# Soft-MoE dispatch after attention: the sum of weights as a 513th column, a minimum on GpSimd, left logits copied by ScalarE, and a new order

## The chip, the cores and the metric

The kernel runs on one NeuronCore of a Trainium2 chip. The core has five engines with a queue each, which meet only through semaphores: PE (TensorE, matrix products, with weight loads shown apart as PEld), DVE (VectorE), ACT (ScalarE), POOL (GpSimd) and SP (SyncE, which here only issues DMA transfers). Each engine executes its queue in the order in which the program was built. The metric is the device time of one execution in microseconds, as the median of several runs.

## The reference

The input is an attention block with a batch of 8, 8 heads, 576 positions and a head width of 64, followed by a soft mixture of experts. All data are float32.

```python
scores = scale * np.matmul(q, k.transpose(0, 1, 3, 2))
thresh = np.max(scores, axis=-1, keepdims=True) - tau
scores = np.where(scores >= thresh, scores, -1000000000.0)
attn = softmax(scores);  x = (attn @ v), laid out as 4608 tokens x 512
logits = x @ phi                              # 4608 x 32 slots
d = np.exp(logits - logits.max(0));  d /= d.sum(0) + 1e-09
slot_input = d.T @ x                          # 32 x 512
for e in range(8): slot_out[e] = np.maximum(slot_input[e] @ w1[e], 0.0) @ w2[e]
c = np.exp(logits - logits.max(1));  c /= c.sum(1) + 1e-09
return c @ slot_out
```

The softmax `d` runs over all 4608 tokens of a slot. The kernel forms it batch by batch: it keeps a running extreme of the logits, a running sum of weights and a running weighted sum of x, and rescales both sums when the extreme moves.

## The kernel before, in words

Attention is done for 32 pairs of heads (`pair(p)`, L1350), four pairs to a batch. A pair has nine row tiles. For each, PE multiplies queries by keys (L1423, L1428 for the last tile) into a PSUM region; DVE copies the scores negated to SBUF and takes their minimum with them (L1435); ACT exponentiates (L1447); POOL computes the threshold from the minimum (`thr`, L1450); DVE masks the exponentials by the threshold and sums them (L1453); PE transposes the result (L1323), ACT copies it out (L1328), and PE multiplies by the values (L1569, L1581, L1594). Only PE, DVE and ACT reach PSUM; there are four regions of two banks for everything (`REGIONS = 4`).

After the fourth pair of a batch comes `dispatch(b)` (L1667). PE computes the logits of the batch for 32 slots (L1688), four column groups wide. DVE copies them negated and takes their minimum (`l4` and one column of `M`, L1694). For every batch but the first, a DVE reduction over the two columns of `M` gives the new running minimum (L1698), and ACT computes the factor `f` by which older sums shrink (L1700). ACT exponentiates the logits (L1702) to weights `dT`, PE transposes them, ACT copies them to `d`. The logits themselves are transposed too and stored for the later softmax over slots: ACT copies those of the 512 main positions (L1712), DVE those of the 64 left positions (L1714), both from one region.

`weigh` (L1731) then forms a weighted sum: four products beside each other and smaller ones for left positions (L1738, L1743), and one DVE operation that merges the region into an accumulator, a copy for the first batch (L1749), else old times `f` plus new (L1751). It is called once with a column of ones, for the sum of weights (`csum`, 128x1, L1754), and once with x (`acc`, 128x512); for the last batch the second is cut into two halves of 256 columns. Each call takes a PSUM region of its own.

After the last dispatch the sums are normalized (`scale`, `slot_in`), and the tail begins: eight experts in two groups (`stage1` L1944, `stage2` L1987), whose weights SP loads. Thirteen slots are filled in small pieces during attention (L1283); the rest is loaded in whole units (L1297, L1302, L1304), each as soon as the buffers that it overwrites are free. The last step combines and writes the output (`combine`).

The order of all this is not the order of the code. `Order.add` records every operation with its engine, an estimated duration, its buffers and a due time. `plan` (L1062) picks again and again the engine whose next operation can start first; among the operations of one engine the due time decides, and due times come from `TABLE`, a table of some thousand numbers by scope and index. It also assigns the PSUM regions and buffer slots. `run` then emits the operations in that order. So a change of the table or of one operation moves neighbours on every engine.

## Time and profile before

| what | value |
|---|---|
| device time, median of 3 runs | 527.16 us (526.46 to 528.51) |
| device time of the profiled execution | 527.1 us |
| its span, first to last instruction | 525.3 us |
| busy in the span: PE / DVE / ACT / POOL | 508.0 / 466.1 / 449.1 / 274.2 us |
| attention, 13.1 to 450 us: PE / DVE / ACT / POOL busy | 435.96 / 427.35 / 415.02 / 259.73 us |
| granted PE clock, mean of the span | 0.991 |

The span is about 1.8 us shorter than the device time, which also holds what lies around the first and last instruction. The attention part, with seven of the eight dispatches in it, fills the first 450 us. From about 452 to 491 us the DMA engines are full with expert weights, and the rest is the last products and the output. A group line of the profile gives a source line, engine, operation and shape, the count, then busy time and mean duration, then the idle time of the engine just before these instructions and what ended it.

### The profile page before, as it was taken

The numbers are of one execution on the slowest core, as the hardware profiler recorded it, in microseconds if no ns is written. First come the engines' busy times: TensorE is split into PE (matmuls) and PEld (weight loads), VectorE is DVE, ScalarE is ACT, GpSimd is POOL, SyncE is SP. The second block draws the span as 40 slices with busy tenths as digits, with TensorE's granted clock in tenths as the row PEclk, the third lists the DMA queues.
The fourth block names the chain that finished last, engine by engine and source line by source line (L and its number), as shares of the span: only waits on it lengthen the run. The fifth ranks groups of instructions, "written<-read, shape, count | busy, mean of one in ns | idle before, by whom it ended". The sixth has DMA issues, their size and how long they took to land.

```text
span 525.3 us, 26986 instructions
## 1 busy us (share of the span) xinstructions
PE 508.0 (97%) x11367; PEld 404.2 (77%) x11367; DVE 466.1 (89%) x1316; ACT 449.1 (85%) x759; POOL 274.2 (52%) x476
## 2 busy tenths in 40 slices
PE   8999999999999999999999999999999999999881
PEld 5778888878978887888788888888788888643361
DVE  6999998999999999999999999999999999623372
ACT  3899998999999998999899989999999999622272
POOL 2555674465656665656466545765466646121110
PEclk9999999999999999999999999999999999999987
DMA  6344553474356533554665553653645334999598
GB/s 170 90 122 105 142 137 99 117 179 126 93 134 162 146 81 98 159 129 133 168 159 144 144 125 106 190 149 96 181 106 161 84 93 138 371 418 416 203 374 345
DMA packets 47817, 86.62 MB, mean 165 GB/s; under 512 B 11344, under 2 KB 31440, under 8 KB 46160
## 3 DMA queue, kind: packets, MB, share of 16 engines
q1 hardware_dynamic: 47376, 84.45, 54.3%
q8 instruction: 89, 1.46, 1.2%
q10 hardware_dynamic: 320, 0.44, 0.3%
q14 instruction: 32, 0.26, 0.2%
HBM read 75.43 MB, written 9.44 MB: 162 GB/s over the span
## 4 chain that ended last, share of the span: by engine, by line
PE 90%; DMA 2%; DVE 2%; ACT 2%; issue 1%; POOL 0%; DVEq 0%; POOLq 0%; ACTq 0%
PE ps L1423 25%; PE ps L1569 21%; PE ps L1323 19%; PE ps L1594 4%; PE ps L1428 4%; PE ps L1581 3%; PE h L1944 3%; PE ps L1688 2%; DMA w<-in_w 2%; PE ps L1630 2%; PE ps L1738 2%; PE o L2038 2%; PE ps L1536 1%; DVE ss L1435 1%; PE so L1987 1%
## 5 line engine op out<-in xcount | busy, mean ns | idle before, releaser
L1435 DVE TENSOR_SCALAR_CACHE_REDUCE ss<-ps 128x576 f32<-128x576 f32 x288 | 208.4, 750 | 8.2 <-PE ps L1423 3.4
L1450 POOL TENSOR_SCALAR thr<-nmx,pabs 128x1 f32<-128x1 f32 x288 | 146.4, 514 | 123.7 <-DVE ss L1435 119.8
L1453 DVE SCALAR_TENSOR_TENSOR p<-ss,thr,p 128x576 f32<-128x576 f32 x256 | 203.9, 821 | 0.5 <-POOL thr L1450 0.2
L1447 ACT ACTIVATE p<-ss,nmx 128x576 f32<-128x576 f32 x256 | 190.2, 786 | 11.5 <-DVE ss L1435 10.3
L1423 PE MATMUL ps<-k,q 64*128 64x288 f32 x1024 | 158.0, 425 | 0.7 <-DVE k L1387 0.7
L1323 PEld LDWEIGHTS ps<-ident,p 64*128 64x128 f32 x2304 | 91.5, 138 | 18.3 <-issue 3.0
L1423 PEld LDWEIGHTS ps<-k,q 64*128 64x128 f32 x1024 | 86.5, 188 | 23.1 <-ACT pTa L1328 2.3
L1323 PE MATMUL ps<-ident,p 64*128 64x64 f32 x2304 | 101.8, 223 | 0.3 <-ACT pTa L1328 0.2
L1328 ACT COPY pTb<-ps 128x1024 f32<-128x1024 f32 (+1 forms) x96 | 83.4, 881 | 2.6 <-PE ps L1323 2.1
L1328 ACT COPY pTa<-ps 128x1024 f32<-128x1024 f32 x64 | 65.4, 1023 | 1.7 <-PE ps L1323 1.4
L1569 PE MATMUL ps<-pTb,vv 64*64 64x128 f32 x1984 | 61.1, 270 | 0.0
L1569 PE MATMUL ps<-pTa,vv 64*64 64x128 f32 x1984 | 60.5, 271 | 0.0
L1569 PEld LDWEIGHTS ps<-pTb,vv 64*64 64x64 f32 x1984 | 56.3, 133 | 2.4 <-ACT pTb L1328 0.5
L1569 PEld LDWEIGHTS ps<-pTa,vv 64*64 64x64 f32 x1984 | 54.8, 133 | 2.8 <-DVE ss L1435 1.0
L1625 POOL TENSOR_TENSOR x<-x,ri 128x512 f32<-128x512 f32 x31 | 38.0, 1225 | 14.1 <-ACT x L1328 12.4
L1478 POOL TENSOR_SCALAR pL<-pL,ri 128x576 f32<-128x576 f32 x31 | 27.6, 891 | 14.7 <-DVE ri L1477 11.0
L1387 POOL TENSOR_SCALAR k<-k,flag 128x576 f32<-128x576 f32 x31 | 29.7, 959 | 2.6 <-PE ps L1323 1.4
L1328 ACT COPY pTl<-ps 128x256 f32<-128x256 f32 x64 | 27.9, 436 | 0.9 <-PE ps L1323 0.8
L1581 PE MATMUL ps<-pTl,vv 64*64 64x128 f32 x496 | 27.0, 278 | 0.0
L1608 ACT COPY xT<-ps 128x256 f32<-128x256 f32 x62 | 23.5, 379 | 4.1 <-PE ps L1594 1.9
L1447 ACT ACTIVATE pL<-ss,nmx 128x576 f32<-128x576 f32 x32 | 25.3, 791 | 1.8 <-DVE ss L1435 1.8
L1453 DVE SCALAR_TENSOR_TENSOR pL<-ss,thr,pL 128x576 f32<-128x576 f32 x32 | 26.0, 814 | 0.1
(194 smaller groups left out, 638.0 us busy)
## 6 DMA issues: line engine op xcount, KB each, us to landing
q<-in_qT SPq DMA_DIRECT2D x62, 288.0 KB, 4.0
w<-in_w SPq DMA_DIRECT2D x52, 256.0 KB, 3.9
host<-in_w SPq DMA_DIRECT2D x10, 1024.0 KB, 8.9
k<-in_kT SPq DMA_DIRECT2D x62, 144.0 KB, 3.9
vv<-in_vt SPq DMA_DIRECT2D x62, 128.0 KB, 3.5
out<-host SPq DMA_DIRECT2D x9, 768.0 KB, 4.3
w<-in_w SPq DMA_DIRECT2D x5, 1024.0 KB, 9.2
vx<-in_vt SPq DMA_DIRECT2D x62, 64.0 KB, 2.9
```

Of the source, the lines that this page charges most:

```text
L1323: nc.tensor.transpose(out=s[:, g, c:c + 64], in_=ins[g], identity=ident[rows[g], rows[g]], tile_position=(64 * g, 0))
L1328: G.add("ACT", 51 + 0.833 * n, nom, lambda: nc.scalar.copy(*io()), r, w)
L1387: sc = lambda e, kc=kc: lambda: e.tensor_scalar(out=kt.t[:, kc], in0=kt.t[:, kc], scalar1=flag8, **one)
L1423: nc.tensor.matmul(s.t[:, g, 0:HS], qt.t[rows[g], h, c * 128:(c + 1) * 128], kt.t[rows[g], h * HS:(h + 1) * HS], start=True, stop=True, ti ...
L1435: dve(678, t + OFF['mx'], [s], [ss, nmx], lambda s=s, ss=ss, nmx=nmx: nc.vector.tensor_scalar(out=ss.t.rearrange("p (a k) -> p a k", a=2), ...
L1447: G.add("ACT", 684, t + OFF['ex'], lambda sv=sv, nmx=nmx, view=view: nc.scalar.activation(view(), sv(), AF.Exp, bias=nmx.t, scale=-1.0), [ ...
L1450: pool(250, t + OFF['th'], pre=75, fn=lambda nmx=nmx, thr=thr: nc.gpsimd.tensor_scalar(out=thr.t, in0=nmx.t, scalar1=1.0, scalar2=pabs, op ...
L1453: fn=lambda sv=sv, thr=thr, view=view, i=i: nc.vector.scalar_tensor_tensor(out=view(), in0=sv(), scalar=thr.t, in1=view(), op0=ALU.is_le, ...
L1478: pool(725, t + OFF['sc'], lambda: nc.gpsimd.tensor_scalar(out=pL.t[:, SL:SL + S], in0=pL.t[:, SL:SL + S], scalar1=ri.t[:, 8:9], **one), [ ...
L1569: nc.tensor.matmul(area(w, h, l)[rows[a]], vv.t[rows[h], n * 64:(n + 1) * 64], pT.t[rows[h], n // 4, n % 4, a * 128:(a + 1) * 128], tile_p ...
L1581: nc.tensor.matmul(area(ab[l], h, l)[rows[a]], vv.t[rows[h], SM:S], pTl.t[rows[h], (l * 2 + a) * 128:][:, 0:128], tile_position=(64 * h, 6 ...
L1625: G.add("POOL", 1040, u + 6.8, own=f"new{j}" + group(b), r=[ri], w=[x[j]], fn=lambda: nc.gpsimd.tensor_tensor(out=wide(), in0=wide(), in1= ...
```

## The change

There are four edits. The two accumulators become one tile `sums` of 513 columns, `acc` and `csum` being views of it. For all batches but the last, the call of `weigh` for the sum of weights goes; its five products now stand ahead of those for x, write the first column of the second bank of the same region, and one DVE operation merges 513 columns. The smaller of the two minima is taken by a POOL `tensor_scalar` instead of a DVE reduction. The logits of the left positions are copied by ACT instead of DVE. And the table of due times is new in nearly every entry; two of its lines are shown here.

```diff
--- before.py
+++ after.py
@@ -57,926 +57,923 @@
 TABLE = {}
 for _n, _v in (
     ("load", [
-        75668,
+        72728,
     ]),
...
@@ -1233,8 +1230,8 @@
     lmain = [lall[:, row(b):row(b) + 4] for b in range(B)]
     lleft = lall[:, N9 - 1:NR:N9]
     crow = cp.tile([128, NR], F32, name="crow")
-    acc = cp.tile([128, DM], F32, name="acc")
-    csum = cp.tile([128, 1], F32, name="csum")
+    sums = cp.tile([128, DM + 1], F32, name="sums")
+    acc, csum = sums[:, 0:DM], sums[:, DM:]
     rs = cp.tile([128, 1], F32, name="rs")
     stn = cp.tile([128, 32], F32, name="stn")
     nabs = cp.tile([128, 1], F32, name="nabs")
@@ -1695,8 +1692,9 @@
             out=l4.t[:, 0:192], in0=lone(wl)[:, 0:192], scalar1=-1.0, scalar2=3.4028234663852886e38, op0=ALU.mult, op1=ALU.min,
             accum_out=M.t[:, 0:1] if b else new.t[:, 1:2]))
         if b > 0:
-            dve(69, u + 1.4, [M], [new["run"]], lambda: nc.vector.tensor_reduce(
-                out=new.t[:, 1:2], in_=M.t, axis=AX.X, op=ALU.min))
+            G.add("POOL", 250, u + 1.4, lambda: nc.gpsimd.tensor_scalar(
+                out=new.t[:, 1:2], in0=M.t[:, 0:1], scalar1=M.t[:, 1:2], scalar2=1.0, op0=ALU.min, op1=ALU.mult),
+                [M], [new["run"]], pre=75)
             G.add("ACT", 200, u + 1.5, lambda: nc.scalar.activation(
                 f.t, M.t[:, 1:2], AF.Exp, bias=new.t[:, 1:2], scale=-1.0), [M["run"], new["run"]], [f])
         G.add("ACT", 319, u + 1.6, lambda: nc.scalar.activation(
@@ -1711,8 +1709,8 @@
         ptr(2, u + 2.5, [l4], [w], lambda w=w: both(w, l4))
         G.add("ACT", 158, u + 2.8, lambda w=w: nc.scalar.activation(
             lmain[b].rearrange("p (g c) s -> p g (c s)", g=2), w.t[:, :, 0:64], AF.Copy, scale=-1.0), [w], [lm[b]])
-        dve(215, u + 2.9, [w], [ll[b]], lambda w=w: nc.vector.tensor_scalar(
-            out=lleft[pl, b // 2], in0=w.t[rows[1], 0, 64:64 + NS], scalar1=-1.0, scalar2=None, op0=ALU.mult))
+        G.add("ACT", 110, u + 2.9, lambda w=w: nc.scalar.activation(
+            lleft[pl, b // 2], w.t[rows[1], 0, 64:64 + NS], AF.Copy, scale=-1.0), [w], [ll[b]])
         if b == B - 1:
 
             w = Buf("s")
@@ -1728,12 +1726,17 @@
                 fs[:, 1:2], new.t[:, 1:2], AF.Exp, bias=fs[:, 0:1], scale=-1.0), [new["run"], fb[0]], [fb[1]])
             dve(96, u + 5.8, [fb[1]], [sb], lambda: nc.vector.tensor_scalar(
                 out=msel[:, 0], in0=st1, scalar1=fs[:, 1:2], scalar2=None, op0=ALU.mult))
-        def weigh(c0, cn, n, rhs, lrhs, dst, pd, dur, nom):
+        def weigh(c0, cn, n, rhs, lrhs, dst, pd, dur, nom, total=False):
 
 
             w = bank_of(b == B - 1)
+            area = lambda: w.t.rearrange("p a n -> p (a n)")[:, 0:n + total]
 
             def mm(w=w):
+                for c in range(5 if total else 0):
+                    nc.tensor.matmul(
+                        w.t[c % 4 * 32:c % 4 * 32 + 32, 1, 0:1], d.t[:, c * NS:(c + 1) * NS], ones_left if c == 4 else ones,
+                        start=c < 4, stop=c > 0, tile_position=(0, 32 * (c % 4)), skip_group_check=True)
                 for c in range(4):
                     nc.tensor.matmul(
                         lone(w)[c * 32:(c + 1) * 32, 0:n], d.t[:, c * NS:(c + 1) * NS], rhs(c), start=True,
@@ -1746,12 +1749,15 @@
             rd = ([] if n == 1 else [x, xl]) + [d]
             G.add("PE", dur, nom, mm, rd, [w], mode=COLS4, more=116 if n > 1 else -60)
             if b == 0:
-                dve((65 if n > 1 else 126) + n * 1.17, nom + 1, [w], [pd], lambda: nc.vector.tensor_copy(dst, lone(w)[:, 0:n]))
+                dve((65 if n > 1 else 126) + n * 1.17, nom + 1, [w], pd, lambda: nc.vector.tensor_copy(dst, area()))
             else:
-                dve((65 if n > 1 else 126) + n * 1.17, nom + 1, [w, f], [pd], lambda: nc.vector.scalar_tensor_tensor(
-                    out=dst, in0=dst, scalar=f.t, in1=lone(w)[:, 0:n], op0=ALU.mult, op1=ALU.add))
-
-        weigh(0, 1, 1, lambda c: ones, lambda c: (slice(0, 1), ones_left), csum, cs, 192, u + 6)
+                dve((65 if n > 1 else 126) + n * 1.17, nom + 1, [w, f], pd, lambda: nc.vector.scalar_tensor_tensor(
+                    out=dst, in0=dst, scalar=f.t, in1=area(), op0=ALU.mult, op1=ALU.add))
+
+        if b == B - 1:
+            weigh(0, 1, 1, lambda c: ones, lambda c: (slice(0, 1), ones_left), csum, [cs], 192, u + 6)
+        else:
+            G.skip(2)
         pieces = 2 if b == B - 1 else 1
         n = 512 // pieces
         if pieces == 2:
@@ -1759,8 +1765,8 @@
         for g in range(pieces):
             q = slice(g * n, (g + 1) * n)
             weigh(g * 2, 4 // pieces, n, lambda c, q=q: x.t[:, c, q], lambda c, q=q: (
-                slice(c * 128 - q.start, c * 128 + 128 - q.start), xl.t[:, c * 128:c * 128 + 128]), acc[:, q],
-                ac[g] if pieces == 2 else ac, 1101 / pieces, u + 7)
+                slice(c * 128 - q.start, c * 128 + 128 - q.start), xl.t[:, c * 128:c * 128 + 128]), acc[:, q] if pieces == 2 else sums,
+                [ac[g]] if pieces == 2 else [ac, cs], 550.5 if pieces == 2 else 1200, u + 7, pieces == 1)
         if pieces == 2:
             slot_in()
 
```

The first place is the queue of DVE in the dispatch of the fourth batch, before. `M` holds the two minima, `lall` the stored logits, `acc` and `csum` the sums; `ss`, `nmx`, `thr`, `p` belong to attention.

```order
L1694 TENSOR_SCALAR ss_174,M_150<-ps_307 128x192
L1477 RECIPROCAL ri_278<-ri_278 128x9
L1698 TENSOR_REDUCE M_146<-M_150 128x1
L1453 SCALAR_TENSOR_TENSOR p_206,r_274<-ss_134,thr_230,p_206 128x9x64
L1714 TENSOR_SCALAR lall<-ps_309 64x32
L1435 TENSOR_SCALAR ss_134,nmx_270<-ps_307 128x576
L1435 TENSOR_SCALAR ss_154,nmx_250<-ps_309 128x576
L1453 SCALAR_TENSOR_TENSOR p_206,r_274<-ss_126,thr_226,p_206 128x9x64
L1453 SCALAR_TENSOR_TENSOR p_234,r_274<-ss_134,thr_242,p_234 128x9x64
L1751 SCALAR_TENSOR_TENSOR acc<-acc,f_130,ps_307 128x512
L1751 SCALAR_TENSOR_TENSOR csum<-csum,f_130,ps_309 128x1
L1435 TENSOR_SCALAR ss_126,nmx_258<-ps_310 128x576
```

The same place of DVE's queue now (lines of the changed kernel are three lower here).

```order
L1691 TENSOR_SCALAR ss_173,M_153<-ps_309 128x192
L1432 TENSOR_SCALAR ss_125,nmx_249<-ps_306 128x576
L1450 SCALAR_TENSOR_TENSOR p_233,r_273<-ss_133,thr_229,p_233 128x9x64
L1450 SCALAR_TENSOR_TENSOR p_245,r_273<-ss_125,thr_225,p_245 128x9x64
L1432 TENSOR_SCALAR ss_173,nmx_257<-ps_306 128x576
L1474 RECIPROCAL ri_277<-ri_277 128x9
L1450 SCALAR_TENSOR_TENSOR p_245,r_273<-ss_149,thr_221,p_245 128x9x64
L1432 TENSOR_SCALAR ss_133,nmx_269<-ps_308 128x576
L1450 SCALAR_TENSOR_TENSOR p_233,r_273<-ss_173,thr_241,p_233 128x9x64
L1754 SCALAR_TENSOR_TENSOR sums<-sums,f_129,ps_309 128x513
L1432 TENSOR_SCALAR ss_149,nmx_237<-ps_307 128x576
```

The reduction of `M`, the copy into `lall` and the second merge are gone from the queue; between the logits' minimum and the merge there are only attention's operations and a reciprocal.

The second place is the queue of POOL in the same dispatch, now; `M` is new there, `thr` are the thresholds, `pL` scores of left queries and `ri` reciprocals.

```order
L1447 TENSOR_SCALAR thr_229<-nmx_249,pabs 128x1
L1472 TENSOR_SCALAR ri_201<-r_273 128x9
L1695 TENSOR_SCALAR M_153<-M_145 128x1
L1447 TENSOR_SCALAR thr_221<-nmx_257,pabs 128x1
L1447 TENSOR_SCALAR thr_229<-nmx_269,pabs 128x1
L1611 TENSOR_TENSOR xT_169<-pTb_185 128x64
L1475 TENSOR_SCALAR pL_213<-pL_213,ri_201 128x576
```

The minimum has entered between a small operation and two thresholds; before, this queue held only attention's operations there.

The third place is PE's queue at the weighted sums of the same dispatch, before.

```order
L1323 MATMUL ps_308<-ident,p_210 128x64 x16
L1738 MATMUL ps_307<-x_138,ss_174 32x512 x4
L1743 MATMUL ps_307<-xl_142,ss_174 32x128 x4
L1738 MATMUL ps_309<-ones,ss_174 32x1 x4
L1743 MATMUL ps_309<-ones_left,ss_174 32x1
L1423 MATMUL ps_310<-k_282,q_286 128x288 x2
```

And PE's queue there now.

```order
L1320 MATMUL ps_306<-ident,p_205 128x64 x16
L1737 MATMUL ps_309<-ones,ss_125 32x1 x4
L1737 MATMUL ps_309<-ones_left,ss_125 32x1
L1741 MATMUL ps_309<-x_137,ss_125 32x512 x4
L1746 MATMUL ps_309<-xl_141,ss_125 32x128 x4
L1320 MATMUL ps_308<-ident,pL_213 128x64 x8
```

The five products with ones went ahead of those with x and write the same region; their number is the same.

## Rows read from the trace of the kernel before

**Rows 1.** The page: busy time by engine, and the group of thresholds.

```profile
PE 508.0 (97%) x11367; PEld 404.2 (77%) x11367; DVE 466.1 (89%) x1316; ACT 449.1 (85%) x759; POOL 274.2 (52%) x476
...
L1450 POOL TENSOR_SCALAR thr<-nmx,pabs 128x1 f32<-128x1 f32 x288 | 146.4, 514 | 123.7 <-DVE ss L1435 119.8
```

**Rows 2.** Stage table: start:end, length, busy by engine, clock, DMA share, GB/s.

```profile
13.10:450.00 436.90, 435.96 (x10705) 364.55 (x10706) 427.35 (x1212) 415.02 (x694) 259.73 (x438) 1.00 0.50 131
452.00:491.00 39.00, 38.04 (x475) 16.48 (x475) 14.49 (x47) 11.77 (x27) 8.52 (x24) 1.00 1.01 415
```

**Rows 3.** Chain of waits from 13.1 to 441 us, shares by line.

```profile
by line: PE ps L1423 29.9%; PE ps L1569 25.8%; PE ps L1323 22.5%; PE ps L1594 4.5%; PE ps L1428 4.2%; PE ps L1581 3.8%; PE ps L1688 2.4%; PE ps L1630 2.3%; PE ps L1738 1.8%; issue 0.9%; ACT pTa L1328 0.7%; PE ps L1743 0.4%; ACT p L1447 0.3%
```

**Rows 4.** Groups of DVE from 13.1 to 450 us: busy us, mean ns, idle before.

```profile
L1751 DVE SCALAR_TENSOR_TENSOR acc<-acc,f,ps 128x512 f32<-128x512 f32 x6 | 4.5, 744 | 0.5 <-PE ps L1743 0.5
...
L1714 DVE TENSOR_SCALAR lall<-ps 64x32 f32<-64x32 f32 x7 | 1.4, 194 | 1.2 <-ACT lall L1712 1.0
L1751 DVE SCALAR_TENSOR_TENSOR csum<-csum,f,ps 128x1 f32<-128x1 f32 x6 | 1.3, 210 | 0.0
...
L1698 DVE TENSOR_REDUCE M<-M 128x1 f32<-128x2 f32 x6 | 0.9, 150 | 0.1
```

**Rows 5.** Timeline in the fourth dispatch: start us, us, instruction, idle before it.

```profile
255.79 0.14 DVE L1698 TENSOR_REDUCE M<-M 128x1 f32<-128x2 f32 x1
...
255.85 0.81 DVE L1453 SCALAR_TENSOR_TENSOR p<-ss,thr,p 128x576 f32<-128x576 f32 x1
...
259.20 0.96 POOL L1387 TENSOR_SCALAR k<-k,flag 128x576 f32<-128x576 f32 x1 [0.69 <-PE ps L1323]
...
259.47 1.29 DVE L1453 SCALAR_TENSOR_TENSOR p<-ss,thr,p 128x576 f32<-128x576 f32 x1
...
260.14 0.22 PE L1738 MATMUL ps<-ones,ss 128*32 128x1 f32 x8
...
260.34 1.90 PE L1423 MATMUL ps<-k,q 64*128 64x288 f32 x12
...
260.69 0.74 DVE L1751 SCALAR_TENSOR_TENSOR acc<-acc,f,ps 128x512 f32<-128x512 f32 x1
261.35 0.20 DVE L1751 SCALAR_TENSOR_TENSOR csum<-csum,f,ps 128x1 f32<-128x1 f32 x1
261.48 0.74 DVE L1435 TENSOR_SCALAR_CACHE_REDUCE ss<-ps 128x576 f32<-128x576 f32 x1
```

**Rows 6.** Groups of the whole run by shape: the merge of 256 columns.

```profile
L1751 DVE SCALAR_TENSOR_TENSOR acc<-acc,f,ps 128x256 f32<-128x256 f32 x2 | 0.9, 470 | 0.0
```

**Rows 7.** Timeline near 442 us: thresholds on POOL, alone and under a DVE instruction.

```profile
441.94 0.27 POOL L1450 TENSOR_SCALAR thr<-nmx,pabs 128x1 f32<-128x1 f32 x1 [1.49 <-DVE ss L1435]
442.36 0.08 DVE L1435 DVE_READ_ACCUMULATOR ss<-ps 128x1 f32 x1
442.36 0.82 DVE L1453 SCALAR_TENSOR_TENSOR p<-ss,thr,p 128x576 f32<-128x576 f32 x1
...
442.61 0.69 POOL L1450 TENSOR_SCALAR thr<-nmx,pabs 128x1 f32<-128x1 f32 x1 [0.41 <-DVE ss L1435]
```

**Rows 8.** Waits of DVE from 13 to 450 us: us in total, times, longest.

```profile
DVE p L1453 <- POOL thr L1450: 0.2, 1, 0.2
```

**Rows 9.** Groups of ACT from 13.1 to 450 us, by shape.

```profile
L1608 ACT COPY xT<-ps 128x256 f32<-128x256 f32 x62 | 23.5, 379 | 4.1 <-PE ps L1594 1.9 <-PE ps L1581 1.0 <-PE ps L1569 0.4
L1612 ACT COPY pTb<-ps 128x128 f32<-128x128 f32 x31 | 8.4, 273 | 0.5 <-PE ps L1594 0.2
```

**Rows 10.** Idle weight loads (PEld) from 13 to 450 us that maxima of DVE ended.

```profile
PEld ps L1323 <- DVE ss L1435: 3.2, 13, 0.4
...
PEld ps L1423 <- DVE ss L1435: 2.2, 8, 0.4
```

**Rows 11.** Timeline of SP at the end of attention: the large weight loads.

```profile
449.34 11.73 SPq L1302 DMA_DIRECT2D host<-in_w  x7
```

**Rows 12.** Waits of SP from 444 to 500 us.

```profile
SPq L1302 <- PE h L1944: 9.7, 3, 6.3
```

More of the change, by code (lines that the diff above doesn't have):

```diff
@@ L773 @@
     ]),
     ("load1", [
-        47742.2,
+        89197.9,
     ]),
     ("load2", [
-        -3701.6,
+        62271,
     ]),
     ("load3", [
-        48185.7,
+        152527.4,
     ]),
     ("load4", [
-        5745.5,
+        19532.5,
     ]),
     ("load5", [
-        -13486.5,
+        36372.5,
     ]),
     ("load6", [
-        45574.8,
+        40270.4,
     ]),
     ("load7", [
-        -8987,
+        47360.4,
     ]),
     ("load8", [
-        -4317.8,
+        27337.9,
     ]),
@@ L798 @@
     ("load9", [
-        13211.2,
+        33807.9,
     ]),
     ("load10", [
-        53227,
+        115810.4,
     ]),
     ("load11", [
-        -5974.3,
+        48436.3,
     ]),
     ("load12", [
-        70422.4,
+        143286.1,
     ]),
     ("load13", [
-        31899.3,
+        41532.9,
     ]),
     ("load14", [
-        -10405.2,
+        19561.3,
     ]),
     ("load15", [
-        29701.9,
+        74202.4,
     ]),
     ("load16", [
-        -5694.7,
+        12067.9,
     ]),
@@ L822 @@
     ("load17", [
-        -6284.7,
+        12657.9,
     ]),
     ("load18", [
-        45578.1,
+        67252.4,
     ]),
     ("load19", [
-        3206.9,
+        67842.4,
     ]),
     ("load20", [
-        56616.6,
+        112419.2,
     ]),
     ("load21", [
-        57206.6,
+        106529.2,
     ]),
     ("load22", [
-        62111.9,
+        55880.6,
     ]),
     ("load23", [
-        96587.7,
+        174484.6,
     ]),
     ("load24", [
-        26541.6,
+        95191.2,
     ]),
@@ L846 @@
     ("load25", [
-        2560.6,
+        68984.1,
     ]),
     ("load26", [
-        38647.9,
+        120473.6,
     ]),
     ("load27", [
-        49640.9,
+        111180.7,
     ]),
     ("load28", [
-        -10517.4,
+        41909.1,
     ]),
     ("load29", [
-        40206.4,
+        123584.1,
     ]),
     ("load30", [
-        441.9,
+        37616.7,
     ]),
     ("load31", [
-        -4948.1,
+        22428.6,
     ]),
     ("load32", [
-        -9190.6,
+        50690.2,
     ]),
@@ L870 @@
     ("load33", [
-        36856.2,
+        96509.1,
     ]),
     ("load34", [
-        12322.7,
+        89039.6,
     ]),
     ("load35", [
-        -18512.1,
+        14011.7,
     ]),
     ("load36", [
-        15591.2,
+        -6020.8,
     ]),
     ("load37", [
-        29959.2,
+        84467.1,
     ]),
     ("load38", [
-        38449.7,
+        88174.6,
     ]),
     ("load39", [
-        25093.7,
+        109168.6,
     ]),
     ("load40", [
-        12741.2,
+        80509.1,
     ]),
@@ L894 @@
     ("load41", [
-        -13283.8,
+        36839.1,
     ]),
     ("load42", [
-        -10006.3,
+        34949.6,
     ]),
     ("load43", [
-        -13058.3,
+        40859.6,
     ]),
     ("load44", [
-        19038.2,
+        58931.1,
     ]),
     ("load45", [
-        9895.2,
+        52814.1,
     ]),
     ("load46", [
-        852.7,
+        13164.6,
     ]),
     ("load47", [
-        31037.8,
+        53778.6,
     ]),
     ("load48", [
-        48109,
+        36036.1,
     ]),
@@ L918 @@
     ("load49", [
-        -13879.8,
+        -14530.9,
     ]),
     ("load50", [
-        -1469.9,
+        24903.6,
     ]),
     ("load51", [
-        45086.4,
+        26673.6,
     ]),
     ("load52", [
-        -16202.4,
+        11941.1,
     ]),
     ("load53", [
-        9327.3,
+        9581.1,
     ]),
     ("soft", [
-        -31759.2, -23404.3, -4440.9, -2032.8, -804.1, -301.3,
+        -31144.9, -22917.2, -4203.7, -2393.8, -1165.2, 2750.1,
     ]),
```

314 lines of the change are left out of this document (157 added, 157 removed), and 471 rows, old and new, of the table TABLE.

## The prediction

> **What bounds the kernel now.** I read the busy line of the page first, then the stage table, then the chain, then the groups and the timeline of one dispatch. The page gives PE 508.0 us of a span of 525.3, DVE 466.1, ACT 449.1 and POOL 274.2 [rows 1]. That is a mean over unlike stages, so the second view cuts out the attention stage. In its 436.9 us PE is busy 435.96, DVE 427.35 (98%), ACT 415.02 (95%) and POOL 259.73 (59%); from 452 to 491 us the DMA engines are at a share of 1.01 and PE is busy 38.04 of 39 [rows 2]. So there are two regimes: attention, where PE and DVE are both nearly full, and a tail whose clock is the arrival of expert weights. The change lies in the first, and in the tail's first 15 us.
>
> Which of PE and DVE is the bound of the first regime decides the forecast. The chain of waits from 13 to 441 us is almost wholly matmul lines, the first three alone 78%, with under 1% of "issue" [rows 3]. But matmul ends are modelled and pipelined, and "PE busy" also counts an operand that arrives late under the matmul before it. DVE's idle time in the stage is 436.90 - 427.35 = 9.55 us, 2%.
>
> The Trainium skill's page "Perfetto Trace Analysis" (Identifying the Most-Contended Engine) says that matmul busy time is a poor measure of PE's headroom and that the busy share of weight loads is to be used, for the vector engines plain occupancy. By it PE stands at 364.55 of 436.9, 83%, DVE at 98%, and DVE alone would be the bound; that is the first rival below. The chain disagrees, and no row settles it, so I give neither the whole.
>
> **The change part by part.** It touches eight dispatches; seven of them (batches 0 to 6) lie in the attention stage, the eighth in the tail.
>
> *The sum of weights leaves DVE.* Six merges of a 128x1 column go from the stage, 210 ns each by their row [rows 4], and for the first batch one copy. What they hold up is less, since DVE starts the next instruction early: the merge of the sum over x starts at 260.69, that of the weights at 261.35, the next instruction at 261.48 [rows 5]. So one costs 0.13 us, seven 0.9 us. The wide merge gets a 513th column: 512 columns take 744 ns [rows 4], 256 take 470 [rows 6], so 1.07 ns each, 0.01 us in all.
>
> On PE the same five products of ones and weights remain; they only move ahead of the sum over x, into the second half of the same PSUM region. Before, they begin at 260.14 and the next score matmul at 260.34 [rows 5], 0.2 us each time. I take the move at nothing, between -0.1 and +0.1 each (-0.7 to +0.7 for seven): in the one case the small products hide in the wide one, in the other they stand alone as before and the wide one begins later. What they gain is a PSUM region: one of four instead of two is held per dispatch.
>
> *The smaller of two minima leaves DVE.* Six reductions (batches 1 to 6) of 150 ns [rows 4]; the example holds its queue from 255.79 to 255.85, 0.06 us [rows 5]. So between 6 x 0.06 = 0.4 and 6 x 0.15 = 0.9 us; I take 0.4, the measured distance between starts. On GpSimd the nearest row is a threshold, an operation of the same form on one column: 0.27 us when alone, 0.69 when it starts under a scalar_tensor_tensor of DVE [rows 7]. Before it stands the hand-over from DVE, 442.44 (end of an accumulator read) to 442.61, 0.17 us [rows 7]. Seven times 0.27 to 0.69 is 1.9 to 4.8 us on an engine that is 436.90 - 259.73 = 177 us idle in the stage [rows 2]. In GpSimd's queue thresholds and the scaling of leftover weights stand behind the waiting minimum; for thresholds DVE waits, ACT's exponential of the dispatch waits for the minimum itself. DVE waited for thresholds 0.2 us in all [rows 8], so they are mostly early, which is the cover. The exponential comes 0.3 to 0.7 us later; PE's queue has other work between it and the products that read it. If that cover is gone, see the third rival.
>
> The Trainium skill, "SBUF — State Buffer" (Who interferes with whom), says that a DVE instruction with two SBUF inputs and a GpSimd instruction that reads SBUF exclude each other, the later one waiting for the whole of the other. Rows agree in both directions: the threshold at 442.61 takes 0.69 instead of 0.27 under the DVE instruction at 442.36 [rows 7], and the DVE instruction at 259.47 takes 1.29 instead of 0.82, begun while GpSimd scales keys [rows 5]. By the rule each minimum could cost DVE up to the same, 6 x 0.47 = 2.8 us, and the DVE saving would be gone.
>
> *The copy of the left logits moves to ACT.* Seven DVE instructions of 194 ns, 1.4 us, and with them waits for the ACT copy that the order puts just ahead, 1.2 us idle [rows 4]. ACT gets seven 64x32 copies: 256 columns take 379 ns, 128 take 273 [rows 9], 0.83 ns a column, so 32 columns are some 0.19 us and seven 1.4 us, against 436.90 - 415.02 = 21.9 us of idle time of ACT [rows 2]. Lower bound 0, upper bound that of the 128-column copy, 2.0 us.
>
> *Sum on DVE:* 0.9 + 0.4 + 1.4 = 2.7 us of work, 3.9 us with the waits that go.
>
> *The order.* Every table entry changes, so what stands next to what is new everywhere. Over the whole attention part PE passes from scores or transposes to products with the values 67 times before and 65 times after; the wide products come at the same places of its queue. So PE's own work is the same, and it can only gain what it waits. Its weight loads stood idle for DVE's maxima 3.2 + 2.2 us at transposes and scores [rows 10], part of that under running matmuls. I take 0 for the order itself, with -2 and +2 as bounds, a bit under half of those waits gained or added.
>
> *The last dispatch and the tail.* SP begins to issue the large weight loads at 449.34 [rows 11], when the last pair frees its buffers; from there DMA is full until 491 [rows 2]. The last minimum's new hand-over (0.3 to 0.7 us) lies under this stream: SP itself waits 9.7 us there for first-layer products of the experts [rows 12] without the DMA engines running dry. So the tail is moved, not shortened: what the attention stage gives, the whole gives.
>
> **Sum.** The profiled execution took 527.1 us (span 525.3 and 1.8 around it), the median of the three runs is 527.16, so they are the same. PE's bound gives 0, DVE's gives -3.9. Both engines are within 2% of full, and each one's idle time is mostly the other's doing, so I take the half, -2.0: 525.1 us.
>
> **Rivals.** A measurement of this kernel can tell about 0.5%, 2.6 us, from no change: faster means under 524.5, slower over 529.8.
>
> First, DVE is the only bound. Then 3.9 us come in full, 527.1 - 3.9 = 523.2; and where the new order also closes the half of the other 8.3 us of DVE's idle time, 519 at the far end. For it: DVE is at 98% of the stage [rows 2]; against it: the chain of rows 3, in which DVE has no share among the large ones.
>
> Second, PE is the only bound, and the change moves work between engines that wait for it: 527.1, bounds 526 to 528 by the order's ±1 us. For it: 435.96 of 436.90; against it: the 5.4 us of idle weight loads that DVE's maxima ended [rows 10].
>
> Third, slower: the minimum blocks GpSimd's queue. Where it is waiting on DVE (0.17) and runs under a two-input DVE instruction (0.69), the threshold behind it is 0.86 us late. If nothing covers that, DVE stands still 6 x 0.86 = 5.2 us, and the ACT copies add 1.4 where ACT is then late: +5.2 + 1.4 - 2.7 = +3.9, 531.0. It decides from (2.64 + 2.7 - 1.4) / 6 = 0.66 us of DVE wait per minimum. For it: GpSimd's thresholds average 514 ns [rows 1], nearly twice the 0.27 of one alone, so they are often held already. Against it: 0.2 us of waiting for thresholds in the whole stage [rows 8]; the queue has room for a late one.
>
> **How the numbers follow.** Forecast 0.43, with a range of its own of 523.5 to 526.7; DVE alone 0.25; PE alone 0.22; the blocked queue 0.10. About a quarter of the first, 0.11, lies under 524.5. So faster 0.25 + 0.11 = 0.36, same 0.32 + 0.22 = 0.54, slower 0.10. The range goes from 521.8 (a bit past DVE alone) to 528.4 (PE alone with a poor order).
>
> **What would show it.** In the new profile: merges of 128x513 of about 745 ns and none of 128x1 in the stage; DVE's busy time to the end of attention about 2.7 us less; no idle DVE before copies of left logits; ACT busy up by 1.4 us; GpSimd up by 1.9 to 4.8; DVE's wait for thresholds still under 1 us; and the large weight loads issued about 2 us earlier, with the 525.3 - 449.3 = 76.0 us from there to the end unchanged. If DVE's idle time in the stage grows by what it was relieved of, PE was the bound. If thresholds become the longest wait of DVE, the third rival was right. If the distance from the first large load to the end changes by over 1 us, my reading of the tail was wrong.

## The result, and the profile after

The changed kernel takes 531.19 us (median of 6 runs, 528.86 to 532.16) beside 527.39 for the kernel before, a ratio of 1.0064, 95% interval 1.0037 to 1.009. So it is slower by 3.8 us, and the forecast of 525.1 with its range of 521.8 to 528.4 missed. The profiled execution took 529.42 us, 2.3 more than the profiled one of before; what follows places these 2.3 in the trace and looks for their cause with runs.

The stage table, as in [rows 2], with the stretch from 13.1 to 450 us and the one that the weights fill:

```profile
13.10:450.00 436.90, 434.59 (x10659) 363.19 (x10659) 424.41 (x1187) 416.03 (x698) 251.22 (x444) 1.00 0.50 131
452.00:491.00 39.00, 38.25 (x479) 17.24 (x479) 14.27 (x46) 13.41 (x29) 7.97 (x24) 1.00 0.99 398
```

SyncE's row that answers to [rows 11], with those of the first three 1 MB loads ahead of it (start, us):

```profile
435.64 0.39 SPq L1294 DMA_DIRECT2D host<-in_w  x1
446.75 2.87 SPq L1294 DMA_DIRECT2D host<-in_w  x2
451.90 11.87 SPq L1299 DMA_DIRECT2D host<-in_w  x7
```

The seven large loads begin at 451.90, not 449.34: attention is 2.56 us longer. From there to the end of the span it is 527.6 - 451.9 = 75.7 us, and was 76.0. So the whole loss of the profiled execution lies in attention, and the tail was only moved.

At 450 us attention is not over in the changed kernel: up to there DVE has done 1212 - 1187 = 25 instructions fewer, and only 20 of them were removed. So the stage is compared up to its own end, the start of the seven large loads, before and now:

```profile
13.10:449.34 436.24, 435.30 (x10699) 364.10 (x10700) 427.18 (x1212) 414.36 (x692) 259.73 (x438) 1.00 0.50 131
13.10:451.90 438.80, 436.39 (x10695) 364.63 (x10694) 426.25 (x1192) 417.93 (x700) 252.46 (x445) 1.00 0.51 132
```

DVE is busy 426.25 us and was 427.18: only 0.93 us are gone, where 2.7 were forecast. Its idle time went from 436.24 - 427.18 = 9.06 to 438.80 - 426.25 = 12.55 us, 3.49 more: the 0.93 of which it was relieved, and the 2.56 by which attention is longer. PE's idle time went from 0.94 to 2.41 us. One reason for 0.93 in place of 2.7 is that rows which stayed got longer; the masks of left queries, before and now, took 0.9 us more in sum:

```profile
L1453 DVE SCALAR_TENSOR_TENSOR pL<-ss,thr,pL 128x576 f32<-128x576 f32 x32 | 26.0, 814 | 0.1
L1450 DVE SCALAR_TENSOR_TENSOR pL<-ss,thr,pL 128x576 f32<-128x576 f32 x32 | 26.9, 842 | 0.2 <-POOL thr L1447 0.2
```

What made them longer no run separates. GpSimd, for which 1.9 to 4.8 us more were forecast, is busy 7.3 us less in spite of the minimum.

The groups of DVE, ACT and POOL from 13.1 to 450 us that answer to [rows 4] and [rows 1] (busy us, mean ns, idle before and its releasers):

```profile
L1450 DVE SCALAR_TENSOR_TENSOR p<-ss,thr,p 128x576 f32<-128x576 f32 x253 | 201.8, 824 | 2.6 <-POOL thr L1447 1.9 <-POOL xT L1611 0.3 <-ACT p L1444 0.2
...
L1754 DVE SCALAR_TENSOR_TENSOR sums<-sums,f,ps 128x513 f32<-128x513 f32 x6 | 4.5, 748 | 0.9 <-PE ps L1746 0.8
...
L1712 ACT ACTIVATE lall<-ps 64x32 f32<-64x32 f32 x7 | 1.4, 194 | 0.1
...
L1447 POOL TENSOR_SCALAR thr<-nmx,pabs 128x1 f32<-128x1 f32 x284 | 139.6, 497 | 100.9 <-DVE ss L1432 95.7 <-DVE ri L1474 0.7 <-DMA vv<-in_vt 0.7
L1384 POOL TENSOR_SCALAR k<-k,flag 128x576 f32<-128x576 f32 x31 | 26.9, 869 | 12.1 <-DMA k<-in_kT 6.1 <-DVE p L1450 3.8 <-PE ps L1425 1.1
L1695 POOL TENSOR_SCALAR M<-M 128x1 f32<-128x1 f32 x6 | 3.7, 620 | 1.8 <-DVE ss L1691 1.7
```

Each price of one operation came out near the forecast: the 513th column costs 748 - 744 = 4 ns (1.07 forecast), the copy on ACT 194 ns, the minimum on POOL 620 ns in the mean, inside 0.27 to 0.69 us. What is new are waits. DVE's longest ones, for [rows 8]:

```profile
DVE ss L1432 <- PE ps L1420: 2.8, 6, 1.2
DVE p L1450 <- POOL thr L1447: 1.9, 7, 0.4
DVE sums L1754 <- PE ps L1746: 0.8, 2, 0.6
```

DVE now waits 1.9 us for thresholds, 0.2 before, and 2.8 us for scores of PE, 1.0 before:

```profile
DVE ss L1435 <- PE ps L1423: 1.0, 4, 0.4
```

In the other direction PE's weight loads for scores now wait 4.7 us for DVE's minima (the maxima of [rows 10], taken of negated scores), where there were 2.2, and twice the products themselves wait:

```profile
PEld ps L1420 <- DVE ss L1432: 4.7, 13, 1.1
PE ps L1420 <- DVE ss L1432: 1.0, 2, 0.6
```

In the chain of waits from 13.1 to 441 us, which before held matmul lines and 1% of ACT [rows 3], DVE and more of ACT and of "issue" now appear:

```profile
by line: PE ps L1420 28.5%; PE ps L1566 24.2%; PE ps L1320 21.0%; PE ps L1591 4.3%; PE ps L1425 3.9%; PE ps L1578 3.5%; PE ps L1627 2.1%; issue 2.1%; PE ps L1685 2.0%; DVE ss L1432 1.6%; PE ps L1741 1.3%; ACT p L1444 1.1%; DVE p L1450 1.0%;
```

### The profile page after: what moved, and what is told of

It reads as the page before. It is cut to its first block, busy times and chain, and to the rows that moved or that the text cites. A ratio compares the mean times of both kernels' runs of the same rounds, so it can differ in the third digit from the quotient of the medians.

```text
span 527.6 us, 27014 instructions
## 1 busy us (share of the span) xinstructions
PE 508.0 (96%) x11367; PEld 404.2 (77%) x11367; DVE 465.4 (88%) x1294; ACT 451.3 (86%) x767; POOL 266.5 (51%) x483
## 4 chain that ended last, share of the span: by engine, by line
PE 85%; DVE 4%; ACT 4%; issue 2%; DMA 2%; POOL 0%; DVEq 0%; POOLq 0%; ACTq 0%
PE ps L1420 24%; PE ps L1566 20%; PE ps L1320 18%; PE ps L1591 4%; PE ps L1425 3%; PE ps L1578 3%; PE h L1950 3%; DMA w<-in_w 2%; PE ps L1685 2%; DVE ss L1432 2%; PE ps L1627 2%; DVE p L1450 1%; PE ps L1741 1%; PE o L2044 1%; PE ps L1533 1%
## 5 line engine op out<-in xcount | busy, mean ns | idle before, releaser
L1447 POOL TENSOR_SCALAR thr<-nmx,pabs 128x1 f32<-128x1 f32 x288 | 141.7, 498 | 108.9 <-DVE ss L1432 103.7
L1384 POOL TENSOR_SCALAR k<-k,flag 128x576 f32<-128x576 f32 x31 | 26.9, 869 | 12.1 <-DMA k<-in_kT 6.1
L1475 POOL TENSOR_SCALAR pL<-pL,ri 128x576 f32<-128x576 f32 x31 | 24.6, 792 | 13.8 <-DVE ri L1474 12.4
```

The lines of the kernel that those rows point to most:

```text
L1384: sc = lambda e, kc=kc: lambda: e.tensor_scalar(out=kt.t[:, kc], in0=kt.t[:, kc], scalar1=flag8, **one)
L1447: pool(250, t + OFF['th'], pre=75, fn=lambda nmx=nmx, thr=thr: nc.gpsimd.tensor_scalar(out=thr.t, in0=nmx.t, scalar1=1.0, scalar2=pabs, op ...
L1475: pool(725, t + OFF['sc'], lambda: nc.gpsimd.tensor_scalar(out=pL.t[:, SL:SL + S], in0=pL.t[:, SL:SL + S], scalar1=ri.t[:, 8:9], **one), [ ...
```

## Experiments

Times are medians; ratios are against the kernel before, timed beside it on the same chip, with the 95% interval. The runs were made in groups on four chips, so runs of different groups are compared by their ratios. 0.1% is 0.53 us. Readings of traces are from one profiled execution of each kernel.

**Edits and order apart.** *edits_alone* is the changed code with the old table, *order_alone* the old code with the new table.

```diff
 # edits_alone: changed code
-TABLE = {...new...}
+TABLE = {...old...}
 # order_alone: old code; the weight sum, which the new table lacks, gets a due time
-    37830.4, None, None, 36850, 38322,
+    37830.4, 37951, 38986, 36850, 38322,   # products +1101, merge +664
```

> The three edits with the table of the kernel before, so that the rows of the two kernels that both issue stand in the old order. Theory A, the new order costs what was lost: the edits keep the forecast's gain, 524.5 to 526.5 us against 527.4 before (ratio 0.995 to 0.998). Rival B, the edits themselves cost it (the minimum on GpSimd ahead of the thresholds, the merge that waits for all products): 529 to 532 us (ratio 1.003 to 1.009), with DVE's idle time before the 513-column merges and before p<-ss,thr,p grown as in the changed kernel.

> The code of the kernel before with the new table; the weight sums, which have no entry there, are put right behind the weighted sums as they stood before. Theory A: 529 to 533 us (ratio 1.004 to 1.01), and the key's wait for its DMA on GpSimd (1.2 us before, 6.1 us after) stays near 6 us. Rival B: 526.5 to 528.5 us (ratio 0.998 to 1.002).

Measured: 532.35 us for each, 1.0094 (1.0073 to 1.0115) and 1.0106 (1.0084 to 1.0129). Both theories fell as I had put them: each half alone costs 5 us or more, both together 3.8. The new order costs the old code some 5.6 us and the edits cost the old order 5, so there is no half to blame; a part of the loss had to be looked for in each.

**One edit at a time, in the old order.** *null* has none of the three, only the two sums as one tile.

```diff
 # only_csum / only_min / only_left: edits_alone with the other two undone, for instance
-        G.add("ACT", 110, u + 2.9, lambda w=w: nc.scalar.activation(
-            lleft[pl, b // 2], w.t[rows[1], 0, 64:64 + NS], AF.Copy, scale=-1.0), [w], [ll[b]])
+        dve(215, u + 2.9, [w], [ll[b]], lambda w=w: nc.vector.tensor_scalar(
+            out=lleft[pl, b // 2], in0=w.t[rows[1], 0, 64:64 + NS], scalar1=-1.0, scalar2=None, op0=ALU.mult))
```

> Only the 513th column, in the old order; minimum and left-logit copies stay on VectorE. The two runs before say that the edits in the old order cost 5 us (532.35 against 526.99), so one or more of them must. Theory C, the 513th column does it, because the sum of the copied weights now holds back the one merge and the bank: 530 to 532 us here, and 526 to 528 in the other two. Rivals M (minimum) and L (left copies): 526 to 527 us here, since seven short merges of 0.13 us each are gone.

> Only the smaller of two minima on GpSimd, in the old order. Theory M, the minimum stands in GpSimd's queue ahead of thresholds that wait for it: 530 to 532 us here, with VectorE's wait for thr grown from 0.2 us to over 1. Rivals C and L: 526.5 to 528 us.

> Only the left logits' copies on ScalarE, in the old order. Theory L, each copy of 0.2 us puts off an exponential that TensorE's transposes wait for: 529 to 532 us here. Rivals C and M: 525.5 to 527.5 us, because VectorE loses seven copies of 194 ns.

> None of the three edits and the old order: only the running sum and its weight sum lie side by side in one tile of 513 columns in place of two. All theories that blame one edit: 526.5 to 527.5 us. If it is at 530 or more, the place of the tiles in memory costs the time, and neither edits nor order.

Measured: only_csum 528.43, 1.0035 (1.0013 to 1.0057); only_min 530.52, 1.0072 (1.0056 to 1.0087); only_left 530.56, 1.0078 (1.0059 to 1.0098); null 527.46, 1.0013 (0.9998 to 1.0027). No single culprit, and the sum of the three, 1.85%, is far over the 0.94% of all. In all but null one row of SyncE's queue had moved: the planner places the first 1 MB load 5 ns ahead of the *planned* start of the last small value load, and with any edit that start shifts. SyncE's rows in edits_alone (start, us):

```profile
448.34 2.57 SPq L1297 DMA_DIRECT2D host<-in_w  x3
...
452.93 11.97 SPq L1302 DMA_DIRECT2D host<-in_w  x7
```

All three 1 MB loads start only at 448.34; in null the first goes out at 433.46 and in the changed kernel at 435.64, under attention. So 1 MB more goes through the stretch in which the DMA engines are full, and from the first large load to the end it is 531.6 - 452.9 = 78.7 us, beside 76.0. In only_csum's profiled execution attention is as long as before (the large loads begin at 449.43), and its loss lies behind it: 526.3 - 449.4 = 76.9 us.

**The load put back.** 

```diff
-        ... NP * N9 + 9 if i else (start[final] - 5) * 9 / PERIOD, ...
+        ... NP * N9 + 9 if i else (start[final] - 4000) * 9 / PERIOD, ...   # 3000 in min_host, 1000 in left_host
```

> The three edits, the old order, and the first 1 MB load of the expert weights put back ahead of the last small value load on SyncE's queue, where it stands in the kernel before. In all kernels so far but the one without edits, the planned start of that small load moved and the 1 MB load fell behind it, from 434 to 445 us and later; their time from the first of the seven large loads to the end is 76.9 to 78.7 us, not 75.6 to 76.0. Theory H, some 2 to 2.7 us of what the edits cost in the old order is this misplaced load, the rest is attention: 529.2 to 530.5 us, with 75.5 to 76.3 us from the first of the seven loads to the end. Rival, the load makes no difference and the end of those kernels is slow for another reason: 531.5 to 533 us.

> Only the minimum on GpSimd, old order, the first 1 MB load back in its place. Theory H: 528 to 529 us, what is left over the 527.5 of the kernel without edits is the longer way from the logits to the exponential (VectorE waited 2.3 us for ScalarE's copy of the logits, 1.0 before). Rival M, the minimum itself costs the 3 us: 530 to 531 us.

> Only the left logits' copies on ScalarE, old order, the first 1 MB load back in its place. Theory H: 528 to 529 us. Rival L, the copies on ScalarE cost the 3 us: 530 to 531 us. Were the forecast's saving of 1.4 us of VectorE work real, 526 us.

Measured: edits_host 530.62, 1.0069 (1.005 to 1.0089); min_host 528.26, 1.0031 (1.0017 to 1.0045); left_host 529.31, 1.0043 (1.003 to 1.0056). Each is 0.25 to 0.41% lower than with the load misplaced, with intervals apart for min_host and left_host and overlapping for edits_host. So the load has a price; but only min_host lies in the range of theory H, the other two are above theirs, and edits_host (529.9 - 452.9 = 77.0 us to the end) got back only a part. What is left lies in attention, but for that 1 us. It also shows the changed kernel's order in another light: with the edits, the new order (1.0064) is no better than the old one (1.0069).

**The minimum undone in the new order.** *undo_min* is the changed kernel with the minimum back on DVE and the first 1 MB load kept in its place.

```diff
-            G.add("POOL", 250, u + 1.4, lambda: nc.gpsimd.tensor_scalar(...), [M], [new["run"]], pre=75)
+            dve(69, u + 1.4, [M], [new["run"]], lambda: nc.vector.tensor_reduce(
+                out=new.t[:, 1:2], in_=M.t, axis=AX.X, op=ALU.min))
```

> The changed kernel with its order, only the minimum back on VectorE (1 MB load in its place). If the minimum on GpSimd costs something of its own in the changed kernel: 529.5 to 530.5 us, faster than its 531.2. If each order fits only the code it was searched with: 531.5 to 534 us, slower than with the minimum on GpSimd.

Measured: 529.95, 1.006 (1.0043 to 1.0076), beside 1.0064 with the minimum on POOL. Neither theory can be told from this: the median lies in the first range, the difference far inside the intervals. It does show that DVE's waits for thresholds came with the order and not with the minimum: with the minimum gone they are still 1.5 us, and 1.6 in order_alone, which has none of the edits.

```profile
DVE p L1450 <- POOL thr L1447: 1.5, 6, 0.4
```

**Is DVE's relief worth anything?** From here the kernel before with all rows in their places, and work left out or added.

```diff
 # without_two: two instructions per dispatch left out, nothing in their place (the left logits are zeroed once, at the start)
-        dve(215, u + 2.9, [w], [ll[b]], lambda w=w: nc.vector.tensor_scalar(...))
+        dve(215, u + 2.9, [w], [ll[b]], lambda: None)
-                dve(..., nom + 1, [w, f], [pd], lambda: nc.vector.scalar_tensor_tensor(
+                dve(..., nom + 1, [w, f], [pd], lambda: None if n == 1 and b < B - 1 else nc.vector.scalar_tensor_tensor(
 # left_twice
+            ... op0=ALU.mult) for _ in range(2)])
```

> The kernel before in its own order, and VectorE's seven merges of the weight sum in the attention stage's dispatches but the first and the last, and all its left-logit copies, are left out with nothing in their place (TensorE still makes the products; the left logits stay zero): 2.3 us less work for VectorE, no other row moved. The forecast's step that relief of VectorE shortens the stage, half of it or all: 524.5 to 526 us. Theory Z, relief of VectorE is worth nothing here, since its waits grow by as much: 526.5 to 527.5 us.

> The kernel before in its own order, each left-logit copy issued twice on VectorE: 1.4 to 1.5 us more work for it, no other row moved. If VectorE bounds the stage with TensorE: 528 to 528.7 us. Theory Z: 526.7 to 527.5 us.

Measured: without_two 527.2, 0.9998 (0.9986 to 1.0011); left_twice 528.78, 1.0024 (1.0011 to 1.0038). The stage row of without_two:

```profile
13.10:450.00 436.90, 435.89 (x10696) 363.79 (x10694) 425.73 (x1199) 414.77 (x693) 260.71 (x438) 1.00 0.51 132
```

```profile
449.38 11.73 SPq L1303 DMA_DIRECT2D host<-in_w  x7
```

DVE's busy time fell from 427.35 to 425.73, and attention did not get shorter: its large loads begin at 449.38, 449.34 before. All 1.62 us came back as idle time. Relief is worth 0, within 0.7 us; the half that the forecast took would be 0.8. Work added is paid nearly in full by the median, 1.3 us for 1.4, but the interval allows 0.6 to 2.0. (The doubled copy also holds its PSUM region longer; in its trace no instruction waits for it.) That relief is not paid back is the forecast's step that failed first. (The expectation speaks of seven merges between the first and the last dispatch; there are six, as [rows 4] has them.)

**What takes its place.** *left_also_act* and *min_also_pool* do the new work on the new engine into a spare tile, beside the old work.

```diff
 # left_also_act
+            nc.scalar.activation(spare[pl, 0:NS], w.t[rows[1], 0, 64:64 + NS], AF.Copy, scale=-1.0)])
 # min_also_pool
+            nc.gpsimd.tensor_scalar(
+                out=spare[:, 0:1], in0=M.t[:, 0:1], scalar1=M.t[:, 1:2], scalar2=1.0, op0=ALU.min, op1=ALU.mult)])
```

> The kernel before in its own order, and ScalarE copies the left logits too, into a spare tile: 1.4 us more work for ScalarE and one more reader of the bank, VectorE's row unchanged. If the copies on ScalarE cost what the run with them alone lost (529.31 against 527.05, in its own order with the load in place): 528.5 to 530 us. If that loss came from VectorE's row being gone and everything shifting: 526.7 to 527.5 us.

> The kernel before in its own order, and GpSimd takes the minimum of the two too, into a spare tile, while VectorE still takes it for use: the queue of GpSimd has six more rows of 0.3 to 0.7 us, but the chain to the exponential is as short as before. If the minimum costs by blocking the thresholds behind it (the forecast's third rival): 528 to 531 us and VectorE waiting for thr over 1 us. If it costs by the longer chain from the logits to the exponential alone: 526.7 to 527.5 us.

Measured: left_also_act 529.88, 1.0053 (1.0033 to 1.0072); min_also_pool 527.31, 1.0002 (0.999 to 1.0014). So the minimum's row in GpSimd's queue is free in the old order, and DVE waits for thresholds as little as before (0.2 us): the forecast's third rival, whose 531.0 us nearly met the result, named the wrong mechanism. In min_also_pool DVE waits 0.6 us for ACT's copy of the logits; in min_host, where the exponential waits for GpSimd, DVE's own left copy stands behind that chain for 2.1 us (1.0 in the kernel before):

```profile
DVE lall L1715 <- ACT lall L1713: 2.1, 3, 1.1
```

The copies on ACT cost 2.8 us for 8 x 0.19 = 1.5 us of work. The timeline of left_also_act in the fourth dispatch shows where a part of that goes, ACT first, then PE:

```profile
256.72 0.29 ACT L1713 ACTIVATE lall<-ps 128x128 f32<-128x128 f32 x1
256.90 1.01 ACT L1329 COPY pTb<-ps 128x1024 f32<-128x1024 f32 x1
257.94 0.19 ACT L1717 ACTIVATE spare<-ps 64x32 f32<-64x32 f32 x1
```

```profile
257.24 0.28 PE L1324 MATMUL ps<-ident,ss 64*128 64x64 f32 x4
258.19 0.76 PE L1424 MATMUL ps<-k,q 64*128 64x288 f32 x4 [0.66 <-ACT spare L1717]
```

Both copies read the PSUM region that holds the transposed logits. In ACT's queue a 1.01 us eviction stands between them, so the region comes free at 258.13; the next scores go into it, and PE stands idle for 0.66 us. In the kernel before, DVE's copy starts as soon as ACT's main copy ends, and the same scores follow 0.33 us behind its start:

```profile
256.94 0.19 DVE L1714 TENSOR_SCALAR lall<-ps 64x32 f32<-64x32 f32 x1 [0.28 <-ACT lall L1712]
...
257.27 0.70 PE L1423 MATMUL ps<-k,q 64*128 64x288 f32 x4
```

Over the stage of left_also_act these wait for the copy on ACT (us, times):

```profile
  PEld ps L1424: 1.1, 2
  PEld ps L1324: 0.9, 2
  PE ps L1424: 0.7, 1
  PEld ps L1740: 0.4, 1
  PE ps L1324: 0.2, 1
```

**The copy placed ahead of the eviction.** 

```diff
 # left_also_early, against left_also_act; edits_early does it with the real copy, in edits_host
         G.add("ACT", 158, u + 2.8, lambda w=w: [nc.scalar.activation(
             lmain[b].rearrange(...), w.t[:, :, 0:64], AF.Copy, scale=-1.0),
+            nc.scalar.activation(spare[pl, 0:NS], w.t[rows[1], 0, 64:64 + NS], AF.Copy, scale=-1.0)], [w], [lm[b]])
```

> As the run in which ScalarE copies the left logits too (529.88 us, 1.0053), with the same rows on every engine, but ScalarE's second copy stands right behind its copy of the main logits, ahead of the 1.01 us eviction that it stood behind. In that run's trace TensorE waited 0.7 and 1.1 us for the copy near 258 us, since the bank of the transposed logits comes free only behind it. Theory K, the late release of the bank is the price: 527.2 to 528.2 us. Rival, ScalarE's 1.4 us of work is the price wherever it stands: 529.3 to 530.5 us.

> All three edits in the old order with the 1 MB load in its place (530.62 us, 1.0069), and the left logits' copy right behind that of the main logits on ScalarE. Theory K: 528 to 529 us, what is left is the longer chain through GpSimd's minimum and the 513th column. Rival: no change, 530 to 531.5 us.

> As the last, with the minimum back on VectorE. If the chain through GpSimd costs 1 us: 527 to 528.2 us, level with the kernel before at 527.2. If VectorE's relief were worth its 1.4 us for once its replacement costs nothing: 525.5 to 526.5 us. If the 513th column costs 1.8 us by itself: 528.5 to 529.5 us.

Measured: left_also_early 528.74, 1.0033 (1.0018 to 1.0048); edits_early 529.38, 1.0043 (1.0024 to 1.0063); edits_early_nomin 528.18, 1.0025 (1.0009 to 1.0041). The first two lie between the ranges of theory K and of its rival. By the medians two fifths come back, 0.20% of 0.53% and 0.26% of 0.69%; the intervals of each pair overlap, so only the direction, twice the same, speaks for theory K. PE no longer waits for the copy: in edits_early nothing does, and in left_also_early, which has both copies, only DVE's own:

```profile
  DVE lall L1716: 1.9, 5
```

The minimum back on DVE gives 0.18% more, about the 1 us expected of its chain, again with intervals that overlap. The fourth dispatch of edits_early shows where its chain ends, in GpSimd, ACT and PE:

```profile
255.00 0.85 POOL L1698 TENSOR_SCALAR M<-M 128x1 f32<-128x1 f32 x1 [0.33 <-DVE ss L1694]
255.88 0.42 ACT L1703 ACTIVATE ss<-ps,M 128x192 f32<-128x192 f32 x1 [0.74 <-POOL M L1698]
256.36 0.76 PE L1423 MATMUL ps<-k,q 64*128 64x288 f32 x4 [0.44 <-ACT ss L1703]
```

The exponential reads the logits from their PSUM region. ACT waits 0.74 us for the minimum before it, and the next scores, which need nothing of the exponential but the region, wait for its end. In the stage PE waits so for 0.8 us, at two places, and not at all in edits_early_nomin. At 1.0025 the 513th column and ACT's early copies are in, and that is 0.12% over null: the 513th column costs little or nothing.

**The new order's late keys.** GpSimd waits 6.1 us for key loads in the changed kernel and 4.8 in order_alone, 1.2 before.

```diff
 # keys_sooner: changed kernel; the first 1 MB load is kept in its place
-        nom = [x[2] * PERIOD / 9 + at(*x) for x in self.noms]
+        nom = [x[2] * PERIOD / 9 + at(*x) - 2500 * (i in self.sooner) for i, x in enumerate(self.noms)]   # the key loads
```

> The changed kernel with its order, where the key loads alone come up to 2.5 us earlier in SyncE's queue. In the new order GpSimd waits 4.8 to 6.1 us for keys (1.2 before) and VectorE 1.9 us for thresholds that stand behind them (0.2 before). If that is what the new order loses: 529 to 530 us and VectorE's waits for thr under 0.6 us. If the loss lies in how the new order staggers the compute engines: 530.5 to 532 us with the waits for keys gone or not.

Measured: 531.79, 1.009 (1.0066 to 1.0113). The wait for keys is gone, that of DVE for thresholds is not, and no time came back:

```profile
POOL k L1386 <- DMA k<-in_kT: 0.4, 1, 0.4
```

```profile
DVE p L1452 <- POOL thr L1449: 2.0, 7, 0.4
```

## Why the prediction was wrong

*DVE's saving, forecast -3.9 and taken at half, -2.0.* This term failed in two steps. From rows to work: the rows did go, but up to the end of attention DVE is busy only 0.93 us less, not 2.7, since others got longer. And from work to time: the experiment without replacement measures it, 0 and not half. There the prediction's own test decides as written, "If DVE's idle time in the stage grows by what it was relieved of, PE was the bound": the idle time grew by the 1.62 us that were left out. In the changed kernel it grew by 3.49 for 0.93, so there the test says only that waits were added. The Trainium skill, "Perfetto Trace Analysis" (Identifying the Most-Contended Engine), would make DVE the engine to relieve, at 98% occupancy against 83% of weight loads; this measurement speaks against it, since taking 427.35 - 425.73 = 1.6 us of busy time from DVE gave nothing. But DVE isn't free either: 1.4 us more cost 1.3. That PE, DVE and ACT pass buffers around nearly without slack, so that work added shows and work removed doesn't, would explain both and was only argued.

*ACT's copies, taken as hidden in 21.9 us of idle time.* They cost 2.8 us added to the old order, 1.7 to 3.8 by the interval. I weighed only the engine's idle time and never asked what a copy releases. The row moved from a queue where it ran as soon as its input was there to one with a 1 us eviction ahead of it, and a PSUM region was held as much longer. Placed ahead of the eviction the copy still cost 1.7 us (1.0033), and what makes up that rest is not shown. In the changed kernel's own order nothing in attention waits for that copy, so there it was placed well and the price of the held region isn't paid.

*The minimum on GpSimd.* That its row would be hidden was right (1.0002). That the exponential could come 0.3 to 0.7 us later at no cost was not: I looked only at who reads its result, and it also releases the logits' PSUM region, for which PE waits 0.8 us in edits_early. Undoing it there gives 0.18%, with intervals that overlap. In the changed kernel no product waits for that exponential. (The working also sets seven minima against attention's idle time; six lie in it, 1.6 to 4.1 us.) The third rival had the right time and sign by a wrong path: DVE's waits for thresholds did grow to 1.9 us, but with the order. The 2.8 us that DVE could lose where a two-input instruction and GpSimd exclude each other, worked out for the rule of the Trainium skill's page "SBUF — State Buffer" (Who interferes with whom), weren't paid: the run with six such rows added costs 0.0002, between -0.5 and +0.7 us. Where the two engines got in each other's way, the time fell on GpSimd: the added minima take 0.79 us in the median and 0.29 at the least, while DVE's masks stay at 822 ns (821 before).

*The 513th column and its products.* 4 ns a merge where 1 was forecast, and with the move of the products and ACT's early copies no more than 0.12% over null, too little to tell.

*The order, taken at 0 with bounds of -2 and +2.* Out of bounds for the old code: +5.6 us (1.0106), of which the profiled execution has 5.0 in attention (large loads at 454.31). For the changed code it's worth about nothing, 1.0064 beside 1.0069 for the same edits in the old order with the load in place. What it changes shows in the waits that the term was sized by: in the four kernels of the new order PE's weight loads wait 3.8 to 4.7 us for DVE's minima at scores and 1.6 to 2.1 at transposes, in all sixteen of the old one 2.0 to 2.3 and 2.9 to 4.0. The two nearly cancel, so their sum doesn't explain the loss.

*The tail moved, not shortened.* Right here (75.7 against 76.0 us), with the first 1 MB load kept ahead by the new order. In five kernels of the study it fell behind; in four of them the tail was 76.9 to 78.7 us, in order_alone 76.3, and put back in three of them it gave 0.25 to 0.41%.

The loss in the old order is thus taken apart from 1.0094 to 1.0025: 0.25% the misplaced load, 0.26% the region held by ACT's late copy, 0.18% the minimum's chain; the rest may be ACT's work and the single tile of null. Each step is near the width of its interval; the direction of all three is what the runs show. What stays open is what the changed kernel loses in its own order: it pays neither for the load nor for the held region, undoing the minimum changes nothing that can be told from noise, and earlier keys don't help. Its waits (DVE 2.8 us for scores, 1.9 for thresholds) are spread over many places, and that the new stagger of the engines causes them was only argued. None of the versions tried beats the kernel before.

## What to carry to other kernels

Before a small instruction is moved to an idler engine, look at the queue that it joins and at the buffer that its end releases: 0.19 us of work behind a 1 us eviction held PE up for 0.66 us. Test what a relief is worth by leaving the work out in the old order; here that run alone would have told that the relief of DVE had nothing to win. Read a stage up to its own end in each kernel: in a window of fixed length idle time grows by whatever the busy time lacks, and of the 427.35 - 424.41 = 2.94 us that DVE seems to save here up to 450 us, 2.0 were work still to come. And compare an edit with the order held fixed row by row, the loads' queue too, since a planner that derives one row's place from another's planned start can move 1 MB out of its cover for a reason that has nothing to do with the edit.

## What had not been expected of the hardware

Two executions in which PE does the same rows in the same order differ by single slips that no wait in the profile accounts for. The same transposes in without_two, then in left_also_early, there with their weight loads and the copy that these are shown to wait for:

```profile
125.86 0.66 PE L1324 MATMUL ps<-ident,p 64*128 64x64 f32 x16
```

```profile
125.50 0.37 ACT L1329 COPY pTl<-ps 128x256 f32<-128x256 f32 x1
...
126.64 0.58 PEld L1324 LDWEIGHTS ps<-ident,p 64*128 64x128 f32 x16 [1.10 <-ACT pTl L1329]
126.64 0.72 PE L1324 MATMUL ps<-ident,p 64*128 64x64 f32 x16 [0.65 <-issue]
```

The copy had ended at 125.87, 0.77 us before the weight loads began. One such slip is a quarter of the effects looked for here (and the twelve runs of null go from 525.90 to 528.48 us), so that a single profiled execution couldn't rank these kernels; only the repeated runs could.
